# Converting the first dense group's third matrix between attention and its first product, and turning expert 0's rows three steps earlier

## The chip, the cores and the metric

The kernel runs on one core of a Trainium2 chip. The core has a matrix engine (TensorE, PE in the profile, with its weight loads shown as PEld), a vector engine (VectorE, DVE), an activation engine (ScalarE, ACT), a general engine (GpSimd, POOL) and SyncE (SP), which here only issues DMAs. Each engine works through its own instructions in order; semaphores make one wait for another. The metric is device time in microseconds of one launch; lower is better.

## The reference

Three parts follow each other: a masked attention, a dense gated layer, and a layer in which every token is sent to one of eight experts or to none.

```python
scores = scale * np.matmul(q, k.transpose(0, 1, 3, 2))        # 4 x 8 heads, 576 x 576, depth 64
mask_local = (rel >= 0) & (rel < 32)                          # heads 0 to 3
mask_strided = (rel >= 0) & (pos[None, :] % 32 == pos[:, None] % 32)   # heads 4 to 7
...
attn = attn / (np.sum(attn, axis=-1, keepdims=True) + 1e-09)
x = np.matmul(attn, v)                                        # then 2304 tokens x 512

gate = 1.0 / (1.0 + np.exp(-(x @ w_gate)))                    # w_gate, w_val 512 x 1536
x = gate * (x @ w_val) @ w_out                                # w_out 1536 x 512

do_compute = x @ w_skip > 0
e_idx = np.argmax(x[do_compute] @ w_gate8, axis=1)            # 8 experts
for e in range(8):
    h = np.maximum(xc[mask] @ w1[e], 0.0)                     # w1[e] 512 x 1024
    y[mask] = gate_w[mask, None] * (h @ w2[e])                # w2[e] 1024 x 512
out[do_compute] = xc + y
```

The three matrices of the dense layer arrive as 64-bit floats, everything else as 32-bit floats.

## The kernel before

All work is written in one fixed order by hand (a manual schedule): the order in which Python emits instructions is the order in which each engine does them. Waits follow from the tiles that are read and written, and from buffers that are used again.

**Precision.** A dense product is made of three: `mm3` (L434 to L436) multiplies high part by high part, high by low and low by high, so a weight and its operand each exist as `h` and `l` tiles (`whg`, `wlg` and so on; `xth`, `xtl` for the attention's result). The weights come as pairs of 32-bit words. `Weights.fetch(i)` (L382) loads one half of a 256 x 512 block (512 KB) by SP; `Weights.convert(i)` makes 32-bit floats of it in five DVE instructions (L396, L399, L402, L405, L409; tiles `cvg`, `cvv`, `cvo`), then ACT makes the high part (L417) and POOL subtracts to get the low part (L413). Since ACT and POOL are to come later in the order, these two are kept in the lists `after_act` and `after_pool` until a `flush`.

**Attention.** 32 steps (two query halves of two heads each) run as a pipeline that a string of letters sets in order: per step PE makes scores (L281), turns the probabilities (L328) and the next q or k (L222, L239) and applies v (L342); DVE, ACT and POOL do maxima, exponentials (L304), scaling (L319), and the high and low parts of the result (L350, L351, L362, L364). From step 13 on, PE also gets *fill* work: half a gated product of group 0 for units 0 to 2 (`gv_raw`, six `mm3` instructions each step). So `w_gate` and `w_val` of group 0 are fetched and converted in attention (letters L and D), and before the change `w_out` of group 0 is too: its halves are fetched at steps 13 and 14 and converted in the steps from 15 on.

**Dense layer.** The 2304 tokens are five units (four of 512, one of 256), the 1536 middle columns six groups of 256. `gv` makes the gate and value products of a unit and group, 48 instructions for two column blocks f; `glu` (L462, L463, L464, L467) makes `gt`, the gated product, in high and low part; `mout` multiplies by `w_out` (`who`, `wlo`) into `acc`. Right after attention come `glu_raw` for units 0 and 1 (sigmoid L506, product L507 on DVE, high part L509, low part L510 on POOL), `gv(0, 3)` for the fourth unit, then `mout` and `gv` in turn. A `tick` between output blocks moves one step of a later group's conversion.

**Choice and experts.** In the last group, each finished unit is turned back to rows (`turn_back`: L734, L735, L737, L738), its expert is chosen (`pick`, L747 to L775: nine small DVE instructions), and a step later its rows are scattered to `xs` by expert (`place`, L796). For the last unit (u = 4), the first 128 rows of expert 0 are fetched (`fetch`, L845, from units 0 to 2) and turned by `prep` (PE L872, ACT L874, DVE L876; tile `xx`) from within its second gated product: `route` is called after each of the four k steps of the gate (`g`) and value (`v`) product. The first expert products (`hide`, L998) and the last `mout` follow.

**Memory.** Pool `slab` has 30 buffers of 4 KB per partition, `slab2` 15 of them, in the memory that attention's tiles (masks, raw q and k, probabilities `pT`) leave.

Of the kernel before, what the change touches and what calls it, by code (L numbers as in the profile page):

```python
# [21 lines left out]
def kernel(  # L22
# [25 lines left out]
    G = 2  # L48
# [9 lines left out]
    NU = -(-NT // UT)  # L58
# [114 lines left out]
    def load_qk(b, ty, hp):  # L173
        if hp == 0:
            r = [att.tile([128, 2, 4, 2, D], F32, tag="raw", bufs=4, name=f"raw_{n}{b}{ty}") for n in "qk"]
            r.append(att.tile([128, 2, 2, D], F32, tag="rem", bufs=2, name=f"rem{b}{ty}"))
            raw_t[b, ty] = r
        r = raw_t[b, ty]
        h0 = 4 * ty + 2 * hp
        for i, src in enumerate((q, k)):  # L180
            for h in range(2):
                nc.sync.dma_start(
                    r[i][:, hp, :, h, :], src[b, h0 + h, 0:512, :].rearrange("(p r) d -> p r d", r=4)
                )
        for i, src in enumerate((q, k)):
            nc.sync.dma_start(
                r[2][64 * hp:64 * hp + 64, i], src[b, h0:h0 + 2, 512:S, :].rearrange("h p d -> p h d")
            )
# [24 lines left out]
    def turn(it, i, warm=0):  # L213
        b, ty, hp = it
        raw = raw_t[b, ty]
        if i == 0:
            kqs[it] = att.tile([128, 2, S], F32, tag="kq", bufs=3, name=f"kq{b}{ty}{hp}")
        kq = kqs[it]
        pt = bank([128, 4, 128], "Y")
        busy(warm, pt)  # L220
        for r in range(4):
            nc.tensor.transpose(pt[:, r, :], raw[i][:, hp, r].rearrange("p h d -> p (h d)"), ident)  # L222
        if ty == 0:
            dst = kq[:, i, 0:512].rearrange("p (c r) -> p c r", r=4)
            src = pt.rearrange("p r c -> p c r")
        else:
            dst = kq[:, i, :].rearrange("p (c r t) -> p c r t", r=4, t=TPC)[:, :, :, 0:16]
            src = pt.rearrange("p r (t c) -> p c r t", c=8)
        if i == 0:
            nc.vector.tensor_scalar(dst, src, SCALE, None, op0=ALU.mult)  # L230
        else:
            nc.scalar.copy(dst, src)
# [190 lines left out]
    after_act, after_pool, glus = [], [], []  # L423

    def flush(jobs):
        todo = list(jobs)
        jobs.clear()
        for job in todo:
            job()

    wt = {}
# [6 lines left out]
    def run(steps, n=99):  # L438
        for _ in range(n):
            if next(steps, 0) == 0:  # L440
                return
# [4 lines left out]
    def gv_mm(g, u, f, nm, tag, step=None):  # L446
        fs = slice(128 * f, 128 * f + 128)
        ps = bank([128, width(u)], tag)
        assert wt[g, nm].ready == 2
        whi, wlo = wt[g, nm].hi, wt[g, nm].lo  # L450
        for kk in range(KD):
            mm3(ps, whi[:, kk, fs], wlo[:, kk, fs], plane(xth[u], kk), plane(xtl[u], kk), kk == 0, kk == KD - 1)
            if step is not None:
                step(nm, kk)
        return ps

    def glu(g, u, f, pg, pvl):
        n = width(u)
        gt = slab2([128, 2, n], F32R, f"gt{g}{u}{f}")
        gts.setdefault((g, u), []).append(gt)  # L460
        sg = late.tile([128, UT], F32, tag="sg", bufs=2, name="sg")[:, 0:n]
        nc.scalar.activation(sg, pg, AF.Sigmoid)  # L462
        nc.vector.tensor_tensor(sg, sg, pvl, op=ALU.mult)  # L463
        nc.scalar.copy(gt[:, 0, :], sg)  # L464

        def low_part():
            nc.vector.tensor_tensor(gt[:, 1, :], sg, gt[:, 0, :].bitcast(F32), op=ALU.subtract)  # L467

        flush(glus)
        if f + 1 < G:  # L470
            glus.append(low_part)
        else:
            low_part()

    def gv_f(g, u, f, step=None):
        glu(g, u, f, *(gv_mm(g, u, f, nm, "ZY"[f], step) for nm in "gv"))

    def gv(g, u):
        for f in range(G):
            gv_f(g, u, f)  # L480

    def gv_raw(u, f, i):
        if i == 0:
            raws[u, f] = slab([128, 2, UT], F32, f"gvr{u}{f}")
        ps = bank([128, UT], "Z")
        w = wt[0, "gv"[i]]
        assert w.ready == 2
        fs = slice(128 * f, 128 * f + 128)
        for kk in range(KD):
            mm3(ps, w.hi[:, kk, fs], w.lo[:, kk, fs], plane(xth[u], kk), plane(xtl[u], kk), kk == 0, kk == KD - 1)  # L490
            if kk == 1:
                yield
        dst = raws[u, f][:, i, :]
        if i == 0:
            nc.vector.tensor_copy(dst, ps)
        else:
            nc.scalar.copy(dst, ps)  # L497
        yield

    def glu_raw(u):  # L500
        for f in range(G):
            raw = raws.pop((u, f))
            gt = slab2([128, 2, UT], F32R, f"gt0{u}{f}")
            gts.setdefault((0, u), []).append(gt)
            sg = raw[:, 0, :]
            nc.scalar.activation(sg, sg, AF.Sigmoid)  # L506
            nc.vector.tensor_tensor(sg, sg, raw[:, 1, :], op=ALU.mult)  # L507
            yield
            nc.scalar.copy(gt[:, 0, :], sg)  # L509
            nc.gpsimd.tensor_tensor(gt[:, 1, :], sg, gt[:, 0, :].bitcast(F32), op=ALU.subtract)  # L510
            yield
# [31 lines left out]
    load_qk(0, 1, 0)  # L543
    load_v(0, 0)
    load_qk(0, 1, 1)
    for nm in "gvo":
        wt[0, nm] = Weights(0, nm, slab, slab)
    ADD = 20
    NRAW = 3
    FILL = {}  # L550
    FILL0 = 13
    BUSY = ((1, 2), (1, 2), (1, 2), (1, 2), (0, 1), (0, 1), (0, 1), (0, 1), (0, 1), (0, 0), (0, 1), (0, 1), (1, 1), (1, 1), (0, 1), (1, 0))
    FETCH = (5, 6, 7, 8, 13, 14)
    halves = [x for u in range(NRAW) for i in range(2) for f in range(G) for x in [gv_raw(u, f, i)] for _ in range(2)]
    for i, x in enumerate(halves):
        FILL.setdefault(min(FILL0 + i, NS + 2), []).append(x)
    early = [(nm, i) for nm in "gvo" for i in range(2)]
    turn(items[0], 0, 8)
    turn(items[0], 1, 1)
    cq = []  # L560
# [59 lines left out]
    def step_loads(t):  # L620
# [16 lines left out]
        if 17 <= t < 23:  # L637
            late_consts(t - 17)
        if t in FETCH:
            nm, i = early[FETCH.index(t)]  # L640
            wt[0, nm].fetch(i)
        if t - 2 in FETCH:
            nm, i = early[FETCH.index(t - 2)]
            cq.append(wt[0, nm].convert(i))
# [24 lines left out]
    def slab2(shape, dt, name):  # L669
        return late.tile(shape, dt, tag="slab2", bufs=NSLAB2, name=name)  # L670
# [236 lines left out]
    for g in range(1, NG):  # L907
        for nm in "gvo":
            plan(g, nm)
    todo = [glu_raw(u) for u in range(NRAW)]  # L910
    for n in range(2 * G):
        for u in range(2):
            run(todo[u], 1)
    gv(0, NRAW)
    for u in range(NU):

        def between(d, u=u):
# [7 lines left out]
    for g in range(1, NG):  # L925
        last = g == NG - 1
        for u in range(NU):
            if g == 2:
                init_xs(u)
            if not last:  # L930
                gv_f(g, u, 0)
                if u > 0:
                    mout(g, u - 1, ticks)
                elif g > 1:
                    mout(g - 1, NU - 1, ticks)
                gv_f(g, u, 1)
                continue
            steps = back = picks = iter(())

            def seat(nm, kk):  # L940
                nonlocal steps
                if u > 1 and (nm, kk) == ("g", 1):
                    steps = place(u - 2, rank_sums(rst[u - 2][1], "X"))
                run(steps, 1)

            gv_f(g, u, 0, seat)
            run(steps)
            if u == 0:
                w_e0.append(load_e(0, 0))
            if u == NU - 1:  # L950
                xg, ins = fetch(0, PARTS[:1])
                tc.add_to_no_dep_group("head", ins.ins)
            if u > 0:
                mout(g, u - 1, part(u - 1))
                back = turn_back(u - 1)
                picks = pick(u - 1)
            else:
                mout(g - 1, NU - 1, ticks)

            def route(nm, kk):  # L960
                if u == NU - 1 and (nm, kk) == ("v", 3):
                    pp.extend(prep(0, xg, PARTS[:1], tag="Z", gates=False))
                if nm == "g":
                    run(back, 2)
                else:
                    run(picks, 4)

            gv_f(g, u, 1, route)
            run(picks)
            for i in {0: (1, 2), 1: (3, 4), 2: (5, 6), 3: (7,)}.get(u, ()):  # L970
                w_e0.append(load_e(0, i))
# [15 lines left out]
    pending, jobs = [], []  # L987
# [297 lines left out]
```

## Time and profile before

| | |
|---|---|
| median of 3 runs | 789.06 us (784.98 to 790.59) |
| profiled execution | 785.84 us, its span 784.1 us |
| PE busy | 757.9 us, 97% of the span |
| DVE, ACT, POOL busy | 487.9, 345.2, 261.6 us |
| granted TensorE clock, mean | 0.994 |

The span runs from the first to the last instruction; the rest of the profiled execution's time lies around it. A busy PE does not mean that PE is at its peak: instructions overlap, and one of 128x512 is listed with 0.39 us where the next begins 0.23 us later. What tells are the places where PE waits, and for whom. All times of rows are from the start of the span.

### The profile page before, as it was taken

How to read it: one execution, taken by the hardware profiler on the slowest of the kernel's cores; microseconds unless marked ns; L12 is line 12 of the kernel's file. 1: busy time of each engine (PE TensorE's matmuls, PEld its weight loads, DVE VectorE, ACT ScalarE, POOL GpSimd, SP SyncE). 2: the span in 40 equal slices, each digit the busy share in tenths (PEclk: the TensorE clock that was granted, in tenths of full speed). 3: DMA queues.
4: the chain of work that ended last, by engine and by line, in shares of the span. 5: the costliest groups of instructions: out<-in, count | busy, mean ns of one | idle time of the engine just before them, and what ended most of it. 6: DMA issues, size and time to landing. Idle time of an engine off the chain costs nothing. (4 is left out here: it accounts for less than half of the span.)

```text
span 784.1 us, 12866 instructions
## 1 busy us (share of the span) xinstructions
PE 757.9 (97%) x4522; PEld 629.0 (80%) x4524; DVE 487.9 (62%) x1130; ACT 345.2 (44%) x1001; POOL 261.6 (33%) x259
## 2 busy tenths in 40 slices
PE   8989999999999999999999999999999999999994
PEld 5757677688888888888888888888888888888882
DVE  4698876469465574575466457277775776665650
ACT  5877679565211221222111212344444755666530
POOL 5565643253111011011011101424424456665610
PEclk9999999999999999999999999999999999999998
DMA  6988451213101333011002000223346766666600
GB/s 162 212 208 220 105 117 32 81 28 108 54 29 52 110 96 122 28 54 54 27 28 81 28 27 27 71 97 135 109 145 185 254 231 234 233 234 207 215 28 13
DMA packets 86447, 87.82 MB, mean 112 GB/s; under 512 B 55991, under 2 KB 58551, under 8 KB 86376
## 3 DMA queue, kind: packets, MB, share of 16 engines
q1 hardware_dynamic: 81032, 76.45, 32.4%
q0 software_dynamic: 3616, 7.33, 2.7%
q10 hardware_dynamic: 1728, 3.15, 1.1%
q8 instruction: 38, 0.62, 0.4%
q14 instruction: 33, 0.27, 0.1%
HBM read 73.48 MB, written 19.28 MB: 118 GB/s over the span
## 5 line engine op out<-in xcount | busy, mean ns | idle before, releaser
L435 PE MATMUL psX<-gt,who 128*128 128x512 f32 (+1 forms) x240 | 88.4, 369 | 0.0
L434 PE MATMUL psX<-gt,who 128*128 128x512 f32 (+1 forms) x240 | 88.4, 368 | 0.0
L464 ACT CAST gt<-sg 128x512 fp32r<-128x512 f32 (+1 forms) x54 | 30.9, 572 | 130.3 <-DVE sg L463 128.8
L436 PE MATMUL psX<-gt,wlo 128*128 128x512 f32 (+1 forms) x240 | 88.3, 368 | 0.0
L319 POOL TENSOR_TENSOR sm<-sm,rs 96x384 f32<-96x384 f32 (+2 forms) x64 | 51.0, 816 | 66.4 <-DVE rs L313 37.0
L528 DVE TENSOR_TENSOR acc<-psX,acc 128x512 f32<-128x512 f32 (+1 forms) x100 | 62.8, 631 | 11.6 <-PE psX L436 11.4
L463 DVE TENSOR_TENSOR sg<-sg,psZ 128x512 f32<-128x512 f32 (+1 forms) x27 | 17.0, 628 | 67.4 <-PE psZ L436 65.8
L413 POOL TENSOR_TENSOR wlv<-cvv,whv 128x512 fp32r<-128x512 f32 x12 | 17.0, 1415 | 113.9 <-ACT whv L417 113.9
L436 PEld LDWEIGHTS psX<-gt,wlo 128*128 128x128 f32 x240 | 45.2, 188 | 7.6
L434 PEld LDWEIGHTS psX<-gt,who 128*128 128x128 f32 x240 | 45.2, 189 | 7.5
L435 PEld LDWEIGHTS psX<-gt,who 128*128 128x128 f32 x240 | 45.2, 188 | 7.5
L434 PE MATMUL psZ<-xth,whv 128*128 128x512 f32 (+1 forms) x132 | 50.3, 381 | 0.9 <-ACT gvr L497 0.7
L434 PE MATMUL psZ<-xth,whg 128*128 128x512 f32 (+1 forms) x132 | 50.3, 381 | 0.0
L436 PE MATMUL psZ<-xth,wlv 128*128 128x512 f32 (+1 forms) x132 | 49.2, 373 | 0.0
L435 PE MATMUL psZ<-xtl,whv 128*128 128x512 f32 (+1 forms) x132 | 49.1, 372 | 0.0
L436 PE MATMUL psZ<-xth,wlg 128*128 128x512 f32 (+1 forms) x132 | 49.0, 371 | 0.0
L435 PE MATMUL psZ<-xtl,whg 128*128 128x512 f32 (+1 forms) x132 | 49.0, 371 | 0.0
L463 DVE TENSOR_TENSOR sg<-sg,psY 128x512 f32<-128x512 f32 (+1 forms) x27 | 17.0, 628 | 47.9 <-PE psY L436 45.7
L1076 POOL DMA_INDIRECT out_dram<-xg x16 | 21.1, 1321 | 75.1 <-DVE xg L1075 40.4
L413 POOL TENSOR_TENSOR wlo<-cvo,who 128x512 fp32r<-128x512 f32 x12 | 17.4, 1450 | 83.4 <-ACT who L417 83.4
L467 DVE TENSOR_TENSOR gt<-sg,gt 128x512 fp32r<-128x512 f32 (+1 forms) x54 | 34.0, 630 | 17.1 <-ACT gt L464 16.6
L413 POOL TENSOR_TENSOR wlg<-cvg,whg 128x512 fp32r<-128x512 f32 x12 | 18.4, 1531 | 71.8 <-ACT whg L417 55.2
(748 smaller groups left out, 2244.5 us busy)
## 6 DMA issues: line engine op xcount, KB each, us to landing
w1r<-in_moe_w_dram SPq DMA_DIRECT2D x32, 512.0 KB
w2r<-in_moe_w_dram SPq DMA_DIRECT2D x32, 512.0 KB
wg<-in_moe_w_gate_dram SPq DMA_DIRECT2D x12, 512.0 KB
wv<-in_moe_w_val_dram SPq DMA_DIRECT2D x12, 512.0 KB
wo<-in_moe_w_out_dram SPq DMA_DIRECT2D x12, 512.0 KB
raw_q<-in_q_dram SPq DMA_DIRECT2D x32, 128.0 KB
raw_k<-in_k_dram SPq DMA_DIRECT2D x32, 128.0 KB
xs<-zero SPq DMA_DIRECT2D x14, 260.5 KB
```

The costliest lines, as they stand in the source:

```text
L319: nc.gpsimd.tensor_tensor(x, x, rs[:n, h, 0:m].rearrange("p (w o) -> p w o", o=1).to_broadcast([n, m, c]), op=ALU.mult)
L413: nc.gpsimd.tensor_tensor(l, wf, h.bitcast(F32), op=ALU.subtract)
L434: nc.tensor.matmul(ps, lhsT=whi, rhs=xhi, start=start, stop=False)
L435: nc.tensor.matmul(ps, lhsT=whi, rhs=xlo, start=False, stop=False)
L436: nc.tensor.matmul(ps, lhsT=wlo, rhs=xhi, start=False, stop=stop)
L463: nc.vector.tensor_tensor(sg, sg, pvl, op=ALU.mult)
L464: nc.scalar.copy(gt[:, 0, :], sg)
L467: nc.vector.tensor_tensor(gt[:, 1, :], sg, gt[:, 0, :].bitcast(F32), op=ALU.subtract)
L528: nc.vector.tensor_tensor(ac, po, ac, op=ALU.add)
L1076: nc.gpsimd.indirect_dma_start(out=out[:, :], out_offset=bass.IndirectOffsetOnAxis(ap=xg[t][:n, TW - 1:TW].bitcast(I32), axis=0), in_=y, i ...
```

## The change

Two things move. First, `w_out` of group 0 is no longer fetched and converted in attention. It is fetched right after attention (into `slab2` buffers, with `row` buffers as scratch), and its conversion runs step by step while the fourth unit's gated products `gv(0, 3)` are emitted: `turn_o` flushes the ACT and POOL lists and moves the conversion one step after each of the 16 k steps. The two DVE, ACT and POOL parts that are left are flushed behind it. Second, for the last unit the turning of expert 0's first rows (`prep`) is called after the first k step of the value product, not after the fourth; the four calls to `pick` of the unit before (the fourth unit) lie behind it now.

```diff
@@ -543,18 +543,18 @@
     load_qk(0, 1, 0)
     load_v(0, 0)
     load_qk(0, 1, 1)
-    for nm in "gvo":
+    for nm in "gv":
         wt[0, nm] = Weights(0, nm, slab, slab)
     ADD = 20
     NRAW = 3
     FILL = {}
     FILL0 = 13
     BUSY = ((1, 2), (1, 2), (1, 2), (1, 2), (0, 1), (0, 1), (0, 1), (0, 1), (0, 1), (0, 0), (0, 1), (0, 1), (1, 1), (1, 1), (0, 1), (1, 0))
-    FETCH = (5, 6, 7, 8, 13, 14)
+    FETCH = (5, 6, 7, 8)
     halves = [x for u in range(NRAW) for i in range(2) for f in range(G) for x in [gv_raw(u, f, i)] for _ in range(2)]
     for i, x in enumerate(halves):
         FILL.setdefault(min(FILL0 + i, NS + 2), []).append(x)
-    early = [(nm, i) for nm in "gvo" for i in range(2)]
+    early = [(nm, i) for nm in "gv" for i in range(2)]
     turn(items[0], 0, 8)
     turn(items[0], 1, 1)
     cq = []
@@ -908,10 +908,23 @@
         for nm in "gvo":
             plan(g, nm)
     todo = [glu_raw(u) for u in range(NRAW)]
+    wt[0, "o"] = Weights(0, "o", slab2, slab3)
+    for i in range(2):
+        wt[0, "o"].fetch(i)
+    first_o = chain(wt[0, "o"].convert(0), wt[0, "o"].convert(1))
+
+    def turn_o(nm, kk):
+        flush(after_pool)
+        flush(after_act)
+        run(first_o, 1)
+
     for n in range(2 * G):
         for u in range(2):
             run(todo[u], 1)
-    gv(0, NRAW)
+    for f in range(G):
+        gv_f(0, NRAW, f, turn_o)
+    for jobs in (after_act, after_pool):
+        flush(jobs)
     for u in range(NU):
 
         def between(d, u=u):
@@ -958,7 +971,7 @@
                 mout(g - 1, NU - 1, ticks)
 
             def route(nm, kk):
-                if u == NU - 1 and (nm, kk) == ("v", 3):
+                if u == NU - 1 and (nm, kk) == ("v", 0):
                     pp.extend(prep(0, xg, PARTS[:1], tag="Z", gates=False))
                 if nm == "g":
                     run(back, 2)
```

On DVE, between attention and the first `mout`, the order before reads as follows (`gvr` is a raw product of `gv_raw`, `sg` the gate of unit 3, `cvg` a conversion for group 1):

```order
L507 TENSOR_TENSOR gvr_1200<-gvr_1200 128x512
L507 TENSOR_TENSOR gvr_1804<-gvr_1804 128x512
L463 TENSOR_TENSOR sg<-sg,psZ 128x512
L463 TENSOR_TENSOR sg<-sg,psY 128x512
L467 TENSOR_TENSOR gt_2525<-sg,gt_2525 128x512
L467 TENSOR_TENSOR gt_2556<-sg,gt_2556 128x512
L396 TENSOR_SCALAR cvg_2579<-wg_2573 128x512
```

The same place on DVE now (`cvo` and `wo` are the third matrix):

```order
L507 TENSOR_TENSOR gvr_1782<-gvr_1782 128x512
L396 TENSOR_SCALAR cvo_2487<-wo_2457 128x512
L399 SCALAR_TENSOR_TENSOR cvo_2487<-wo_2457,cvo_2487 128x512
L402 SCALAR_TENSOR_TENSOR cvo_2487<-wo_2457,cvo_2487 128x512
L405 TENSOR_SCALAR wo_2457<-wo_2457 128x512
L409 SCALAR_TENSOR_TENSOR cvo_2487<-wo_2457,cvo_2487 128x512
L396 TENSOR_SCALAR cvo_2510<-wo_2459 128x512
L399 SCALAR_TENSOR_TENSOR cvo_2510<-wo_2459,cvo_2510 128x512
L402 SCALAR_TENSOR_TENSOR cvo_2510<-wo_2459,cvo_2510 128x512
L463 TENSOR_TENSOR sg<-sg,psZ 128x512
L405 TENSOR_SCALAR wo_2459<-wo_2459 128x512
L409 SCALAR_TENSOR_TENSOR cvo_2510<-wo_2459,cvo_2510 128x512
```

All ten conversion instructions stand behind the last L507, and the first L463 has moved into the second half of them.

On DVE in the last group's last unit, around the choice (L747 to L775) of the unit before, the order before ends the choice like this:

```order
L773 TENSOR_TENSOR eq<-eq,rmx 128x32
L775 TENSOR_TENSOR oh_all<-eq,va 128x32
L876 TENSOR_TENSOR xx_6072<-psZ,xx_6072 128x2x128
L876 TENSOR_TENSOR xx_6073<-psZ,xx_6073 128x2x128
L463 TENSOR_TENSOR sg<-sg,psY 128x256
L467 TENSOR_TENSOR gt_6084<-sg,gt_6084 128x256
```

The same place now:

```order
L876 TENSOR_TENSOR xx_6038<-psZ,xx_6038 128x2x128
L876 TENSOR_TENSOR xx_6039<-psZ,xx_6039 128x2x128
L747 TENSOR_TENSOR lg<-lp 128x40
L759 TENSOR_REDUCE rmx<-lg 128x4
L761 TENSOR_SCALAR va<-lg 128x4
L763 TENSOR_TENSOR eq<-lg,rmx 128x32
L765 TENSOR_TENSOR lm_all<-lg,rmx 128x32
L767 TENSOR_TENSOR eq<-eq,desc 128x32
L771 TENSOR_REDUCE rmx<-eq 128x4
L773 TENSOR_TENSOR eq<-eq,rmx 128x32
L775 TENSOR_TENSOR oh_all<-eq,va 128x32
L463 TENSOR_TENSOR sg<-sg,psY 128x256
```

The two L876 of expert 0's rows have moved from behind the choice to ahead of it; L463 and L467 of the last unit still follow the choice.

On PE at the same place, now:

```order
L735 MATMUL psX<-wri,sl_5918 128x138
L434 MATMUL psY<-xth_2090,whv_4681 128x256
L435 MATMUL psY<-xtl_2091,whv_4681 128x256
L436 MATMUL psY<-xth_2090,wlv_4682 128x256
L872 MATMUL psZ<-ident,xg_5912 128x128 x4
L434 MATMUL psY<-xth_2090,whv_4681 128x256
```

Nine products of the value's remaining k steps come behind the transposes L872; they stood ahead of them.

## Rows read from the trace of the kernel before

**Rows 1.** Who PE waited for, 60 to 100 us: total, times, longest.
```profile
PE psY L239 <- DVE xtl L364: 1.2, 1, 1.2
```

**Rows 2.** Timeline, POOL and DVE in attention: start, us, engine, line.
```profile
86.67 1.48 POOL L413 TENSOR_TENSOR wlo<-cvo,who 128x512 fp32r<-128x512 f32 x1
87.02 1.67 DVE L409 SCALAR_TENSOR_TENSOR cvo<-wo,cvo 128x512 f32<-128x512 int32 x1
88.62 0.76 DVE L364 TENSOR_TENSOR xtl<-psY,xth 128x252 fp32r<-128x252 f32 x2
```

**Rows 3.** Windows: length, busy of the five engines, granted clock, DMA share, GB/s.
```profile
91.70:95.10 3.40, 3.40 (x17) 2.89 (x16) 2.42 (x12) 2.24 (x13) 2.24 (x4) 0.50 0.00 0
```

**Rows 4.** Timeline of PE: starts of fill groups.
```profile
86.63 0.48 PE L434 MATMUL psZ<-xth,whv 128*128 128x512 f32 x1
...
98.20 0.48 PE L434 MATMUL psZ<-xth,whg 128*128 128x512 f32 x1
...
106.51 0.48 PE L434 MATMUL psZ<-xth,whg 128*128 128x512 f32 x1
```

**Rows 5.** Timeline of PE: first and sixth instruction of the first `mout`.
```profile
165.14 0.39 PE L434 MATMUL psX<-gt,who 128*128 128x512 f32 x1
...
166.27 0.39 PE L436 MATMUL psX<-gt,wlo 128*128 128x512 f32 x1
```

**Rows 6.** Timeline of DVE and POOL after attention; x2 merges two instructions, and windows overlap.
```profile
159.53 2.40 DVE L507 TENSOR_TENSOR gvr<-gvr 128x512 f32<-128x512 f32 x2 [1.27 <-ACT gvr L506]
159.65 3.44 POOL L510 TENSOR_TENSOR gt<-gvr,gt 128x512 fp32r<-128x512 f32 x2
161.35 3.00 POOL L510 TENSOR_TENSOR gt<-gvr,gt 128x512 fp32r<-128x512 f32 x2
163.17 0.69 DVE L463 TENSOR_TENSOR sg<-sg,psZ 128x512 f32<-128x512 f32 x1 [1.24 <-ACT sg L462]
```

**Rows 7.** A later conversion on DVE with POOL beside it; last, all copies L417 of `who`.
```profile
187.32 0.42 DVE L396 TENSOR_SCALAR cvo<-wo 128x512 int32<-128x512 int32 x1
187.77 0.69 DVE L399 SCALAR_TENSOR_TENSOR cvo<-wo,cvo 128x512 int32<-128x512 int32 x1
188.62 1.74 POOL L413 TENSOR_TENSOR wlv<-cvv,whv 128x512 fp32r<-128x512 f32 x1 [2.23 <-ACT whv L417]
189.11 1.54 DVE L405 TENSOR_SCALAR wo<-wo 128x512 int32<-128x512 int32 x1
L417 ACT CAST who<-cvo x4: 618/622/632, 82.5 to 195.4; 128x512 fp32r<-128x512 f32 x4
```

**Rows 8.** Window with two fetches of group 1 landing; attention's last product on PE.
```profile
151.00:152.00 1.00, 1.00 (x6) 0.80 (x5) 0.00 (x0) 0.00 (x0) 0.00 (x0) 1.00 1.05 406
...
153.40 0.78 PE L342 MATMUL psY<-pT,v 108*64 108x108 f32 x12
```

**Rows 9.** Timeline of PE and its weight loads in the last group's last unit.
```profile
578.99 0.28 PE L436 MATMUL psY<-xth,wlv 128*128 128x256 f32 x1
580.33 0.42 PEld L872 LDWEIGHTS psZ<-ident,xg 128*128 128x128 f32 x4 [0.20 <-DMA xg<-xs]
582.18 0.39 PE L998 MATMUL psY<-xx,w100h 128*128 128x256 f32 x1 [1.20 <-DVE xx L876]
583.74 0.39 PE L435 MATMUL psX<-gt,who 128*128 128x256 f32 x1
```

**Rows 10.** Timeline of DVE and ACT at the same place.
```profile
579.54 0.20 DVE L747 TENSOR_TENSOR lg<-lp 128x40 f32<-128x40 f32 x1
...
580.89 0.19 DVE L775 TENSOR_TENSOR oh_all<-eq,va 128x32 bf16<-128x32 f32 x1
582.37 0.41 DVE L463 TENSOR_TENSOR sg<-sg,psY 128x256 f32<-128x256 f32 x1
582.82 0.41 ACT L464 CAST gt<-sg 128x256 fp32r<-128x256 f32 x1 [0.86 <-DVE sg L463]
583.25 0.43 DVE L467 TENSOR_TENSOR gt<-sg,gt 128x256 fp32r<-128x256 f32 x1 [0.47 <-ACT gt L464]
```

## The prediction

> **What bounds the kernel now.** TensorE (PE) sets the end. I read first who PE waited for: over the whole span only a few waits reach 1 us. So an edit gains only where it removes a PE wait, and costs only where it makes one. I then read the two places that the change touches, engine by engine, in order of time, and the granted clock beside them.
>
> The first place is the stretch of attention in which `wo` of group 0 is converted. PE's longest wait there, 1.2 us, is for VectorE's (DVE's) L364 [rows 1]. That L364 starts at 88.62 because the conversion's last step, L409, lies before it on DVE: L409 came at 87.02, took 1.67 us, and ended 0.54 us after GpSimd's (POOL's) L413, which had started first and ran from 86.67 to 88.15 [rows 2]. Shortly after this standstill PE runs at the lower of its two clock levels: the granted clock is 0.50 (1.2 GHz) from 91.7 to 95.1 [rows 3].
>
> The second place is the moment at which PE needs `who` and `wlo`. It reads the first half of `who` at 165.14 and the second half of `wlo` at 166.27, and waits for neither [rows 5]: both were done in attention.
>
> **The change part by part.**
>
> *Removed from attention: gain 3.3 us.* From the fill group that begins at 86.63 to the second one behind it, at 98.20, PE took 11.57 us; for the next two, with the same kinds of work between them, it took 8.31 (98.20 to 106.51) [rows 4]. The difference, 3.26, holds the standstill and the slow clock together. At worst only the 1.2 us wait goes away; at best 3.5, with small waits that I don't count. I take 3.3, since both steps consist of the same instructions. Ten DVE instructions, two ACT copies, two POOL subtractions and two 512 KB fetches leave this stretch; the q, k and v loads that SP issued behind them come sooner, and nobody waits long for those, so I count nothing for that. What is late next there is PE's own issue.
>
> *Added between attention and the first `mout`: PE stands still 7.4 us.* The order shows the ten conversion instructions on DVE behind all four L507. The fourth L507 ends at 161.93 (159.53 plus 2.40), and POOL runs L510 without a pause until 164.35: the third of its four starts at 161.35 and ends at 163.09 (159.65 plus 3.44) [rows 6]. PE wants the result 3 to 4 us later. What DVE and POOL do to each other is in rows: POOL's L413 ran from 188.62 to 190.36, and DVE's L405, which came at 189.11 and takes 0.42 alone like L396, ended at 190.65, 0.29 after it [rows 7]; L409 above ended 0.54 after. POOL's operation took 1.74 there instead of about 1.3, because DVE was busy when it came. So, one by one, in the time of the old trace:
>
> - L396 waits for the third L510: 163.09 plus 0.28 is 163.4. The fourth L510 then runs to about 164.6. L399 waits for it: 165.15.
> - L402 (0.69), L405 (0.42) and L409 (0.69) follow free: 166.9 (the durations: [rows 7]).
> - ACT copies the first half of `who` in 0.62 [rows 7]: 167.6. POOL makes the first half of `wlo`, 1.7 with DVE busy: 169.35.
> - Second half on DVE: L396 and L399 to 167.95; L402 is held until `wlo` is done, 169.9; then L463 (0.69 [rows 6]), which stands in the middle of this half, 170.5; L405 and L409 to 171.6.
> - ACT 172.3, POOL 1.3 to 1.4: 173.7.
>
> PE's sixth instruction of `mout` needs this: 173.7 less 166.27 is 7.4 us. In that time PE has five instructions. DVE, ACT and POOL come out of it as far ahead of PE as before, so nothing is given back later. Bounds: if POOL never held DVE, the first half would be ready on DVE at 164.8 and the last step 3.2 us earlier, 4.2; if every step of the second half were held as well, about 8.2.
>
> The page SBUF — State Buffer of the Trainium skill (Who interferes with whom) has the two engines share a port pair as an exclusive lock: the later instruction fully blocks until the first is finished. By that, a held L405 would end its whole 0.42 after POOL's end and a held L409 its 0.69, where the rows show 0.29 and 0.54; over the three held steps of the chain the standstill would be 0.4 longer and the forecast 795.2. I stay with the rows. The same rule speaks against putting a DVE conversion beside POOL's four L510 at all.
>
> *The fetches: nothing.* The first needs the mask's memory, free before the end of attention. The second needs memory that the last attention product still reads, and so is issued at about 154.2 (L342, 153.40 plus 0.78); at the 406 GB/s that SP's queue reached a little earlier, its 512 KB take 1.3 us plus some start-up [rows 8]. DVE comes to it at about 166.9, and the `wg` and `wv` fetches behind it on SP are wanted later still. If that cover were gone, the cost would be added to the 7.4.
>
> *Slow clock after this standstill: 1.7 us.* Five instructions in more than 8 us is less work than PE had in the stretch ahead of 91.7. The row of 91.7 to 95.1 prices one slow stretch: 3.4 us at half speed, 1.7 lost [rows 3]. Bounds 0 (the slow stretch lies inside the standstill) and 3.4 (a second follows); I take one.
>
> *Expert 0's rows turned nine instructions earlier: 1.6 us lost.* The transposes (L872) did not start when PE was free but 0.20 us later, at 580.33, when the rows had landed [rows 9]. The fetch's issue is not moved. So behind the third product of `v` (578.99) PE now waits about 1.1 us for the same landing. That alone costs little: the nine products (1.1 us) fill the 1.2 us in which PE waited for L876 before L998 at 582.18 [rows 9]. But on DVE the two L876 now stand ahead of the choice. The nine instructions of the choice took 579.54 to 581.08, in a time in which DVE had nothing else; now they come behind L876, from about 582.4, where L463 stood [rows 10]. L463 starts at about 583.95, ends at 584.35, ACT's L464 (0.41) ends at 584.8, L467 (0.43) at 585.3. PE's second `mout` product with this tile stood at 583.74 [rows 9]: 1.6 late. Bounds: if the rows landed 1.1 us sooner the choice would start sooner too and the cost is 0 or a gain of some tenths; with a slow clock behind it, 3.3.
>
> *Sum:* -3.3 + 7.4 + 1.7 + 1.6 = +7.4 us. On the profiled execution, 785.84: 793.2. That execution is one of the fast ones: the median of the three runs is 3.2 above it. I add half of that and predict 794.8.
>
> **The rivals.**
>
> *Hidden conversion, not slower.* The place is DVE ahead of the first `mout`. If DVE took the conversion while PE was in the fourth unit's 48 products, the 3.3 stay and only the tail counts: -1.7, 785.7 with the same half added. Decisive is whether the first L396 starts before about 154.5 (7.4 us before 161.9). For it speaks that PE works some 11 us between attention and `mout`; against it, that four L507, each behind an ACT step, stand ahead of it on DVE. Chance 0.06.
>
> *No holding by POOL.* The standstill is 4.2, the clock costs half, the tail is as above: +3.4, 790.8. Against it stand [rows 2, 7]. Chance 0.12.
>
> *Clock falls twice, slower by over 1%.* A second slow stretch, either behind the standstill of 7.4 us or in the tail, where PE now stands twice within 6 us for 1.1 and 1.6 us: +1.7 or, with both, +3.4, so 796.5 to 798.2. Decisive is how much PE does in the stretch before. Against the tail: a wait of 1.2 us at 582 left the clock alone. Chance 0.37.
>
> My forecast has the rest, 0.45.
>
> **How the numbers follow.** About 1% is what a measurement of this kernel can tell from no change. The forecast, 7.4 us, is 0.9% of the mean of the two bases, just inside; the error of the sum (some 1 us) and of a median of runs that spread over 5.6 us put part of it outside, and part of the double-clock case inside. So slower 0.40, within 1% 0.54, faster 0.06. The range takes in the case without holding and the two clock cases with the scatter of the runs: 789.5 to 800; the likeliest case alone is 792 to 797.
>
> **What would show it.** Right: no conversion in attention, fill groups near 4.2 us throughout and no half clock at 92; PE waiting at the first `mout` for `who` from ACT and `wlo` from POOL, some 7 us in total, longer than any wait of before; a stretch of 0.50 behind it; PE waiting about 1 us for `xg` and 1.6 us for the last unit's `gt`. Wrong: conversion steps on DVE that don't stretch while POOL runs; rows of expert 0 that land before the transposes; a half clock in attention that stays although the standstill is gone.

## The result, and the profile after

The changed kernel takes 793.64 us (median of 11 runs, 791.9 to 797.49), the kernel before 785.82 (11 runs, 784.5 to 790.67): ratio 1.0103, 95% interval 1.0081 to 1.0124, which is 8.1 us slower (the medians differ by 7.8). The profiled execution took 797.33 us, its span 795.6; mean granted clock 0.979. Of the 11 executions of the changed kernel four, the profiled one among them, took 796.68 to 797.49 us at a mean granted clock of 0.979 to 0.981, the other seven 791.9 to 794.11 at 0.987 to 0.992.

Who PE waited for in the changed kernel, from 155 to 185 us and from 570 to 600 us (total, times, longest; what is left out waits 0.5 us or less):

```profile
PE psX L434 <- ACT who L417: 4.4, 2, 2.3
PE psX L436 <- POOL wlo L413: 0.4, 1, 0.4
...
PE psZ L872 <- DMA xg<-xs: 1.1, 1, 1.1
PE psX L434 <- ACT gt L464: 1.0, 1, 1.0
```

None of these four stood there before; the 1.2 us for L364 in attention [rows 1] and the 1.2 at L998 [rows 9] are gone. PE's timeline of the changed kernel: two fill groups (answering to 86.63 and 98.20 in [rows 4]), the last product of `gv(0, 3)`, the fourth and sixth of the first `mout` ([rows 5]), and the first of the fifth unit:

```profile
87.06 0.48 PE L434 MATMUL psZ<-xth,whv 128*128 128x512 f32 x1
...
95.25 0.48 PE L434 MATMUL psZ<-xth,whg 128*128 128x512 f32 x1
...
162.01 0.39 PE L436 MATMUL psY<-xth,wlv 128*128 128x512 f32 x1
...
169.12 0.79 PE L434 MATMUL psX<-gt,who 128*128 128x512 f32 x1 [2.07 <-ACT who L417]
...
170.47 0.79 PE L436 MATMUL psX<-gt,wlo 128*128 128x512 f32 x1
...
177.08 0.28 PE L434 MATMUL psZ<-xth,whg 128*128 128x256 f32 x1
```

The fill groups lie 8.19 us apart, 11.57 before. PE could have begun `mout` 0.23 us after 162.01, and in the kernel before the sixth instruction came 1.13 us behind the first [rows 5], so here it could have come at 163.37. It comes at 170.47, 7.1 us later; I call this the standstill. The list above has 4.8 us of it, since it counts only time in which no instruction is listed; in the rest the first five instructions start further apart than before. They are listed with up to 0.79 us in place of 0.39, and the windows (as in [rows 3]) show half the clock, from the time when PE begins again until 175 us, and once more behind the tail. I call such a stretch at 0.50 a half clock.

```profile
164.00:165.00 1.00, 0.28 (x1) 0.29 (x2) 0.96 (x3) 0.95 (x2) 0.26 (x1) 0.92 0.00 0
...
165.00:170.00 5.00, 2.52 (x5) 0.91 (x4) 3.75 (x6) 1.90 (x4) 2.06 (x2) 0.50 0.00 0
...
175.00:176.00 1.00, 1.00 (x6) 0.82 (x5) 0.33 (x1) 0.10 (x1) 0.95 (x1) 0.96 0.00 0
...
602.00:603.00 1.00, 1.00 (x10) 0.91 (x10) 0.22 (x2) 0.27 (x1) 0.99 (x5) 0.50 0.85 224
```

The conversion on DVE in the changed kernel, and POOL beside it (start, us):

```profile
155.54 6.12 POOL L510 TENSOR_TENSOR gt<-gvr,gt 128x512 fp32r<-128x512 f32 x4 [12.07 <-ACT gt L509]
159.01 1.51 DVE L396 TENSOR_SCALAR cvo<-wo 128x512 int32<-128x512 int32 x1
160.56 1.66 DVE L399 SCALAR_TENSOR_TENSOR cvo<-wo,cvo 128x512 int32<-128x512 int32 x1
162.25 0.69 DVE L402 SCALAR_TENSOR_TENSOR cvo<-wo,cvo 128x512 int32<-128x512 int32 x1
...
164.74 1.47 POOL L413 TENSOR_TENSOR wlo<-cvo,who 128x512 fp32r<-128x512 f32 x1 [3.07 <-ACT who L417]
165.11 1.65 DVE L402 SCALAR_TENSOR_TENSOR cvo<-wo,cvo 128x512 int32<-128x512 int32 x1
167.73 0.69 DVE L409 SCALAR_TENSOR_TENSOR cvo<-wo,cvo 128x512 f32<-128x512 int32 x1
169.15 1.28 POOL L413 TENSOR_TENSOR wlo<-cvo,who 128x512 fp32r<-128x512 f32 x1 [2.94 <-ACT who L417]
```

Each step that meets POOL takes 1.5 to 1.7 us, each other 0.42 or 0.69. In the tail, PE and DVE (answering to [rows 9, 10]):

```profile
586.88 0.66 PE L872 MATMUL psZ<-ident,xg 128*128 128x128 f32 x4 [1.09 <-DMA xg<-xs]
588.25 0.76 DVE L876 TENSOR_TENSOR xx<-psZ,xx 128x256 fp32r<-128x256 f32 x2 [2.22 <-ACT xx L874]
588.93 0.19 DVE L747 TENSOR_TENSOR lg<-lp 128x40 f32<-128x40 f32 x1
...
590.38 0.41 DVE L463 TENSOR_TENSOR sg<-sg,psY 128x256 f32<-128x256 f32 x1
591.28 0.38 PE L434 MATMUL psX<-gt,who 128*128 128x256 f32 x1 [1.00 <-ACT gt L464]
```

The choice (L747 on) begins when L876 is done, and L463 waits for the choice to end.

**Where the 11.5 us of the two profiled spans come from.** I subtract the starts of the same PE instruction in the two traces; plus means later in the changed kernel. It is +0.78 at 82 us (it has a half clock at 42 to 45 us that the trace of before lacks, and a longer wait near 49), -2.89 when `gv(0, 3)` begins, +6.49 behind the first `mout`, +6.52 up to the last unit, +8.00 at its last `mout`, +11.39 at the end. So attention gave 3.7, the first `mout` took 9.4, the tail 1.5, and the stretch behind it 3.4, in which the half clock at 598 to 609 lies.

### The profile page after: what moved, and what is told of

Its sections match the earlier page's. It is cut to its first block, busy times and chain, and to the rows that moved or that the text cites. A ratio compares the mean times of both kernels' runs of the same rounds, so it can differ in the third digit from the quotient of the medians.

```text
span 795.6 us, 12870 instructions
## 1 busy us (share of the span) xinstructions
PE 767.2 (96%) x4524; PEld 635.5 (80%) x4524; DVE 488.1 (61%) x1130; ACT 346.3 (44%) x1001; POOL 260.0 (33%) x259
## 5 line engine op out<-in xcount | busy, mean ns | idle before, releaser
L434 PE MATMUL psX<-gt,who 128*128 128x512 f32 (+1 forms) x240 | 90.0, 375 | 5.4 <-ACT who L417 4.4
L436 PE MATMUL psX<-gt,wlo 128*128 128x512 f32 (+1 forms) x240 | 89.8, 374 | 0.6 <-POOL wlo L413 0.4
L435 PE MATMUL psX<-gt,who 128*128 128x512 f32 (+1 forms) x240 | 89.6, 373 | 0.1
L319 POOL TENSOR_TENSOR sm<-sm,rs 96x384 f32<-96x384 f32 (+2 forms) x64 | 49.9, 799 | 68.1 <-DVE rs L313 42.2
L528 DVE TENSOR_TENSOR acc<-psX,acc 128x512 f32<-128x512 f32 (+1 forms) x100 | 62.9, 632 | 11.6 <-PE psX L436 11.4
L463 DVE TENSOR_TENSOR sg<-sg,psZ 128x512 f32<-128x512 f32 (+1 forms) x27 | 17.0, 629 | 66.4 <-PE psZ L436 66.4
L413 POOL TENSOR_TENSOR wlv<-cvv,whv 128x512 fp32r<-128x512 f32 x12 | 16.9, 1409 | 113.9 <-ACT whv L417 113.9
L436 PEld LDWEIGHTS psX<-gt,wlo 128*128 128x128 f32 x240 | 45.9, 191 | 9.7 <-POOL wlo L413 2.0
L436 PE MATMUL psZ<-xth,wlg 128*128 128x512 f32 (+1 forms) x132 | 49.0, 371 | 0.0
L436 PE MATMUL psZ<-xth,wlv 128*128 128x512 f32 (+1 forms) x132 | 49.0, 371 | 0.0
L463 DVE TENSOR_TENSOR sg<-sg,psY 128x512 f32<-128x512 f32 (+1 forms) x27 | 17.0, 629 | 49.1 <-PE psY L436 46.4
L413 POOL TENSOR_TENSOR wlo<-cvo,who 128x512 fp32r<-128x512 f32 x12 | 17.4, 1450 | 89.4 <-ACT who L417 89.4
L467 DVE TENSOR_TENSOR gt<-sg,gt 128x512 fp32r<-128x512 f32 (+1 forms) x54 | 34.1, 631 | 17.0 <-ACT gt L464 16.6
L413 POOL TENSOR_TENSOR wlg<-cvg,whg 128x512 fp32r<-128x512 f32 x12 | 18.4, 1535 | 73.0 <-ACT whg L417 73.0
```

The lines of the kernel that those rows point to most:

```text
L319: nc.gpsimd.tensor_tensor(x, x, rs[:n, h, 0:m].rearrange("p (w o) -> p w o", o=1).to_broadcast([n, m, c]), op=ALU.mult)
L413: nc.gpsimd.tensor_tensor(l, wf, h.bitcast(F32), op=ALU.subtract)
L434: nc.tensor.matmul(ps, lhsT=whi, rhs=xhi, start=start, stop=False)
L435: nc.tensor.matmul(ps, lhsT=whi, rhs=xlo, start=False, stop=False)
L436: nc.tensor.matmul(ps, lhsT=wlo, rhs=xhi, start=False, stop=stop)
L528: nc.vector.tensor_tensor(ac, po, ac, op=ALU.add)
```

## The experiments

All were timed against the kernel before on the same chip; its median was 784.4 to 786.0. The offsets (us, plus is later) are those of the paragraph above, from one profiled execution each, with the half clocks that this one had. "Mout" is a late product of group 0's turn (before: 247.26), "tail" the last unit's last `mout` (586.32).

| version | ratio, 95% interval | gv(0,3) | mout | tail | end |
|---|---|---|---|---|---|
| changed kernel | 1.0103, 1.0081 to 1.0124 | -2.9 | +6.5 | +8.0 | +11.4 |
| e1_matrix_only | 1.0079, 1.0047 to 1.0110 | -3.7 | +5.4 | +5.6 | +7.0 |
| e2_rows_only | 1.0023, 1.0000 to 1.0046 | -1.4 | -1.4 | +1.5 | +3.1 |
| e3_pool_free | 1.0073, 1.0047 to 1.0099 | -3.6 | +2.4 | +4.7 | +8.3 |
| e4_later_in_attention | 0.9995, 0.9974 to 1.0015 | 0.0 | 0.0 | 0.0 | +1.9 |
| e6_choice_first | 1.0002, 0.9985 to 1.0018 | -1.7 | -1.7 | -1.6 | -2.1 |
| e7_conversion_first | 1.0120, 1.0092 to 1.0147 | -2.9 | +7.1 | +7.1 | +6.6 |
| e8_busy_pe | 1.0089, 1.0063 to 1.0115 | -3.9 | +3.4 | +5.9 | +5.7 |
| e9_steps_24_25 | 1.0049, 1.0027 to 1.0070 | -1.0 | -1.0 | -0.9 | +2.4 |
| e10_unit1_in_gv | 1.0099, 1.0069 to 1.0129 | -4.0 | +3.6 | +4.1 | +7.5 |
| e11_units_spread | 1.0061, 1.0041 to 1.0081 | -3.0 | +3.0 | +3.1 | +2.9 |
| e12_fifth_unit_first | 1.0024, 1.0003 to 1.0045 | -3.0 | +1.6 | +1.8 | +1.3 |
| e13_only_order | 1.0045, 1.0025 to 1.0065 | -3.6 | +3.3 | +3.2 | +2.7 |

### Each part alone

The changed kernel with the call of `prep` at `("v", 3)` again:

> The third matrix moved as in the change, expert 0's rows turned behind the fourth k step as before. Theory (two parts that add, the first the larger): about 3.5 us come back in attention and some 9.3 are lost at the first mout (7.2 standing, 2.1 at the slow clock), so 5.7 us slower than the kernel before, and the tail as before, with one wait of 1.2 us at L998 and no slow clock behind it. Rival (the turned rows carry most of the loss): under 3 us slower.

The kernel before with that call at `("v", 0)`:

> Only expert 0's rows turned ahead of the choice; the third matrix is converted in attention as before. Theory: 1.5 us slower than the kernel before, all of it PE's wait for the last unit's gt, since the choice lies behind L876 on DVE; in some executions 3.4 more, when the clock falls behind the two waits. Rival (the wait for the rows only takes the place of the one for L876, and the choice costs nothing): within 0.5 us of the kernel before.

The matrix alone costs 6.2 us by the ratio, the rows alone 1.8; together 8.0, the change 8.1, each with an interval of about 2 us to either side. In e1 attention gave 3.7 and the first `mout` took 9.2, and in the tail only 0.1 changed. In e2 the tail took 3.0, some 1.5 of it by a half clock (584 to 587 us). So the first theory holds. The ratio of e2 (0.0 to 3.6 us) would allow its rival too; it is e2's trace, and the next experiment, that speak for its theory. In e2's attention nothing was changed, and still it lies 1.6 us better from 86.63 to 98.20: the half clock of [rows 3] did not come in that execution.

### The tail: the choice or the wait

The kernel before with

```diff
-                if u == NU - 1 and (nm, kk) == ("v", 3):
+                if u == NU - 1 and (nm, kk) == ("v", 0):
+                    run(picks)
                     pp.extend(prep(0, xg, PARTS[:1], tag="Z", gates=False))
```

> The kernel before, with expert 0's rows turned after the first k step of the value product, but with all of the choice emitted ahead of them, so that DVE's order is that of the kernel before and only PE's transposes move. Theory (the loss in the tail comes from the choice standing behind L876 on DVE, not from PE's wait for the rows): PE waits about 1.1 us for the rows in place of 1.2 at L998, none for gt, and the first product behind the tail comes within 0.3 us of where it stood; total within 0.5 us of the kernel before. Rival (PE's earlier wait is what costs): the tail 1.5 us longer, as in the changed kernel.

PE waits as long for the rows, and for nothing else for longer than before:

```profile
PE psZ L872 <- DMA xg<-xs: 1.2, 1, 1.2
```

The tail takes 0.1 us more than before, and the time is the same. So what the turned rows cost is the choice behind L876 on DVE; PE's earlier wait only takes the place of that at L998.

### What makes the conversion late

The changed kernel, in `glu_raw`, without POOL's subtraction for units 0 and 1 (it leaves out the low parts of these products):

```diff
+            if u < 2:
+                nc.vector.memset(gt[:, 1, :].bitcast(F32), 0.0)
             nc.scalar.activation(sg, sg, AF.Sigmoid)
...
-            nc.gpsimd.tensor_tensor(gt[:, 1, :], sg, gt[:, 0, :].bitcast(F32), op=ALU.subtract)
+            if u >= 2:
+                nc.gpsimd.tensor_tensor(gt[:, 1, :], sg, gt[:, 0, :].bitcast(F32), op=ALU.subtract)
```

> The changed kernel without POOL's four L510 ahead of the conversion: the low parts of the products of units 0 and 1 in group 0 are left out (filled with zeros by DVE while it waits for ACT). Theory (POOL holds DVE): L507 takes some 0.69 us each in place of 1.23 in the second pair, L396 0.42 in place of 1.51, the first L399 0.69 in place of 1.66; the conversion ends 3.4 us sooner, and the time is 3.4 to 5 us under the changed kernel's. Rival (POOL holds nothing, DVE's steps are long for another reason): the steps keep their 1.5 to 1.7 us, and the time is within 0.5 us of the changed kernel's.

DVE in this run, and the first POOL instruction near it:

```profile
158.11 0.41 DVE L396 TENSOR_SCALAR cvo<-wo 128x512 int32<-128x512 int32 x1
158.56 0.69 DVE L399 SCALAR_TENSOR_TENSOR cvo<-wo,cvo 128x512 int32<-128x512 int32 x1
...
161.78 1.47 POOL L413 TENSOR_TENSOR wlo<-cvo,who 128x512 fp32r<-128x512 f32 x1 [19.00 <-ACT who L417]
162.15 1.65 DVE L402 SCALAR_TENSOR_TENSOR cvo<-wo,cvo 128x512 int32<-128x512 int32 x1
```

L396 and L399 take 0.41 and 0.69 with POOL idle, in place of 1.51 and 1.66; the L402 that still meets L413 keeps its 1.65. So POOL does hold DVE. The theory's 3.4 us for the conversion was too much: counted from `gv(0, 3)`, the second `wlo` is done 2.3 us sooner, and the standstill is 4.9 us in place of 7.1. The half clock is shorter as well (166 to 170), so that from `gv(0, 3)` to behind the first `mout` this run loses 6.0 us, the changed kernel 9.4. At the end the ratio has 2.4 us of these 3.4, under the 3.4 to 5 expected, and its interval overlaps that of the changed kernel; its trace has two more half clocks, at 590 to 593 and 600 to 607.

The changed kernel with products in PE's standstill; `warm(k)` emits k products of 128x512 into a bank that nobody reads, and the three products of `mm3` are written out here, so that L436 becomes L536:

```diff
...
+                    warm((10, 11)[f])
+                    nc.tensor.matmul(po, lhsT=ohi[:, f, ds_], rhs=h, start=(f == 0), stop=False)
+                    nc.tensor.matmul(po, lhsT=ohi[:, f, ds_], rhs=l, start=False, stop=False)
+                    warm((4, 0)[f])
...
```

> The changed kernel with 25 further products of 128x512, into a bank that nobody reads, in the places where PE stands still at the first mout (10, 4 and 11 of them); nothing is left out. Theory (the standstill lowers the clock, and that costs 2.1 to 2.3 us on top of it): the granted clock stays at 1.00 from 160 to 176 us, the eighth product row of mout comes 2.1 to 2.3 us sooner than in the changed kernel, and the time is 2 us under it. Rival (the clock falls there for another reason, or the extra products take PE longer than it would have waited): a stretch of 0.50 in spite of them, and the time within 0.5 us of the changed kernel's, or above.

Its windows view for the same five microseconds, and its sixth instruction:

```profile
165.00:170.00 5.00, 4.38 (x18) 2.93 (x17) 3.78 (x7) 2.36 (x4) 1.51 (x2) 1.00 0.00 0
...
169.51 0.50 PE L536 MATMUL psX<-gt,wlo 128*128 128x512 f32 x1 [0.62 <-POOL wlo L413]
```

The last product of `gv(0, 3)` began at 161.02 here, so the standstill, now filled, is still 7.1 us, but the clock stays at 1.00: from the sixth instruction to the fifth unit's first product it takes 4.4 us (to 173.94), against 6.6 in the changed kernel. So the half clock costs 2.2 us, and it comes from PE's standing still: with PE busy it is gone, while e1 and e3, which keep the standstill, have it too (164 to 174 and 166 to 170). Of the 2 us expected in the whole time the ratio shows 1.1, and the two intervals overlap; the trace lost 1.2 us between 530 and 570 us, for which I have no cause.

### Other places in attention

The kernel before with `FETCH = (5, 6, 7, 8, 21, 22)` (e4), and with 24 and 25 at the end (e9):

> The kernel before with the third matrix fetched at steps 21 and 22 of attention in place of 13 and 14, so that it is converted from step 23 on. Theory (in attention the conversion cost 3.7 us only because it met a crowded DVE and POOL near 87 us; later DVE is busy half the time): 3 to 3.7 us faster than the kernel before, no half clock near 92 us, no wait at the first mout. Rival (the conversion costs PE that much wherever it lies in attention): within 0.7 us of the kernel before, with a new wait of over 1 us behind step 23.

> The kernel before with the third matrix fetched at steps 24 and 25 of attention. At steps 21 and 22 the conversion cost PE 3.0 us where it lay, against 3.7 at steps 13 and 14. Theory now (it costs where its last step, held by POOL, stands ahead of an L364 that PE waits for; with DVE busy 2.4 to 2.6 of each 4 us from 123 us on, against 2.3 to 3.6 before that, there is less of it): it costs 1 to 2 us near 125 to 140, so 783.5 to 785 in all. Rival (it costs about 3 us at any place of attention): within 0.7 us of the kernel before.

My theory fell in e4, and the rival came. The old place was 3.7 us shorter, and the new one 3.0 longer. Its windows, with a DVE row and the PE wait behind it:

```profile
119.00:123.00 4.00, 3.08 (x27) 2.61 (x28) 3.93 (x12) 3.85 (x16) 2.95 (x3) 1.00 0.27 83
123.00:127.00 4.00, 2.56 (x29) 1.64 (x28) 3.97 (x22) 2.47 (x10) 1.31 (x3) 1.00 0.00 0
...
122.24 1.67 DVE L409 SCALAR_TENSOR_TENSOR cvo<-wo,cvo 128x512 f32<-128x512 int32 x1
...
124.65 0.72 PE L342 MATMUL psY<-pT,v 128*64 128x96 f32 x12 [0.90 <-DVE xtl L364]
```

DVE is full there, and again an L409 of 1.67 us stands ahead of an L364 for which PE waits, the pattern of [rows 2]; another 1.3 us of waiting there is for POOL's L319. At steps 24 and 25 the loss is 2.6 us, and the pattern is another: the longest wait is for ACT's L332, 1.9 us. So that theory fell too. By the ratio e9 is 3.8 us slower than before, more than its rival allowed; in its trace a half clock at 590 to 600 us lies behind the tail. The half clock near 92 us is no fixed part of the price: e4 lost its 3.0 at a clock of 1.00.

### Attempts to make room for it

In the expectations of this section, "the last version" and "two versions ago" mean e7, and "the version beside it" means e10.

e7, from the changed kernel with `prep` as before, and unit 1's and 2's products from `between`, a unit ahead of the `mout` that reads them:

```diff
-    for n in range(2 * G):
-        for u in range(2):
-            run(todo[u], 1)
+    run(first_o, 2)
+    run(todo[0], 1)
+    run(first_o, 3)
+    run(todo[0], 2)
+    flush(after_act)
+    run(todo[0], 1)
...
-            if u + 2 < NRAW:
-                next(todo[u + 2])
+            if u + 1 < NRAW:
+                next(todo[u + 1])
```

> The third matrix moved as in the change, but its first half is converted right after attention, between the two products of unit 0, the second half behind them, and unit 1's two L507 and L510 come only while unit 0's mout runs; expert 0's rows as before. Theory (PE stands still because the conversion is queued behind four L507 on DVE and collides with four L510 on POOL): both halves are ready some 6 us sooner, PE stands still 1 to 2 us in place of 7.1, the clock stays high or falls for one stretch; of the 3.7 us from attention 1.5 to 3.5 remain, so 782.5 to 784.5 against 786 of the kernel before. Rival (DVE, ACT and POOL have no room there, so the wait only moves): PE waits as long for unit 1's gated product at the second mout, and the time stays over 788.

The first `mout` now loses 1.8 us, as the theory said, but the waits move behind it (160 to 250 us):

```profile
PE psX L435 <- POOL gt L510: 3.8, 3, 2.2
PE psX L436 <- POOL wlo L413: 0.6, 1, 0.6
PE psX L434 <- ACT who L417: 0.5, 1, 0.5
```

With a half clock from 186 to 192 us behind them it is as slow as the change. So the rival was right too. The next two spread these products: in e10 unit 1's over the second block of `gv(0, 3)`, in e11 half of them there and half in the first `mout`, and unit 2's over `gv(0, 4)` (lines of e11, both on top of e7's early conversion):

```diff
+        if kk == 0:
+            run(todo[1], 1)
...
+            for f in range(G):
+                gv_f(0, u + NRAW + 1, f, turn_2)
```

> The last version of the conversion right after attention, but unit 1's two L507 and L510 come while PE is in the second block of the fourth unit's gated products, unit 2's in unit 0's mout as in the changed kernel. Theory (DVE, ACT and POOL have room for all of it from 155 to 190 us; the last version only ran two units' products straight ahead of the mout that reads them): PE stands still 1.8 us at the first mout, under 1 us at the second and third, no slow clock; 3.7 less 1.8 to 2.8 leaves 0.9 to 1.9 us under the kernel before. Rival (there is no room, the wait moves again): waits of over 3 us in all between 160 and 200 us, and over 2 us slower than the kernel before.

> As the version beside it, with unit 1's products half in the fourth unit's second block and half in unit 0's mout, and unit 2's in the fifth unit's gated products. Theory: as for the version beside it, with no wait at the second and third mout; 1.5 to 2 us under the kernel before. Rival (no room): waits of over 3 us in all between 160 and 200 us, and over 2 us slower than the kernel before.

Both theories miss, and both rivals come. The longest wait is now for the bank `psX`. ACT's L526 frees it, and that stands behind the inserted products on ACT: 4.1 us in all in e10, 3.0 in e11:

```profile
PE psX L434 <- ACT acc L526: 4.1, 1, 4.1
...
PE psX L434 <- ACT acc L526: 3.0, 3, 1.5
```

Last, the fifth unit's `gv(0, 4)` ahead of all `mout`s: in e13 that alone (its lines are shown), in e12 with e7's early conversion and with unit 1's products inside `gv(0, 4)`:

```diff
+    gv(0, NRAW + 1)
...
-        if u + NRAW + 1 < NU:
-            gv(0, u + NRAW + 1)
```

> The conversion's first half between unit 0's two products as two versions ago, two steps of its second half ahead of the fourth unit's L463, and the fifth unit's gated products ahead of all of group 0's mouts (unit 1's products while they run, unit 2's in unit 0's mout); expert 0's rows as in the kernel before. Theory (PE stands still because the conversion's result is wanted too soon, and 5.6 us of other products are there to put in between): no wait of 1 us or more for the third matrix at the first mout, no slow clock near it, and the 3 to 3.7 us from attention remain: 781.5 to 783 against 785 of the kernel before. Rival (DVE, ACT and POOL are full, the wait moves to the banks or to a unit's gated product): waits of over 2 us in all from 160 to 200 us, no faster than the kernel before.

> The third matrix moved as in the change, with nothing but the fifth unit's gated products put ahead of group 0's mouts; expert 0's rows as before. Theory (the same, but the fourth unit's L462 and L463 stand among the late conversion, and the fifth unit's products need the banks that these free): PE waits 2 to 3 us for the banks at 162 us and about 1 more at the first mout, in place of 7.2 for the third matrix, with no slow clock or one short stretch; within 1 us of the kernel before. Rival (the third matrix is that late whatever stands between): over 3 us slower than the kernel before.

In e12 PE waits nowhere for the third matrix and the clock stays up, but ACT's L526 is late four times:

```profile
PE psX L434 <- ACT acc L526: 2.7, 4, 1.5
```

It loses 4.6 us between `gv(0, 3)` and the late product, more than these 2.7. Each of the four waits costs some 0.27 us that the list does not count: instructions overlap by 0.16 us where PE does not wait (listed with 0.39, the next 0.23 later), and the first behind a wait takes 0.50. Two pauses too short for the list, near 172 and 175 us, cost 0.7. In e13 the loss is 6.9, with 2.8 us of waiting for L462 and a half clock at 166 to 170. Both theories miss again, and both rivals come. e12 is the nearest, and is still 0.24% slower than the kernel before (0.03 to 0.45). So the third matrix cost PE 2.6 us or more at every other place tried; at its old one it costs 3.7, or 2.1 where the half clock doesn't come.

## Why the prediction was right

*Attention, -3.3.* Measured 3.4 between the two fill groups, 3.7 with the group ahead of them. But 1.6 of it is a half clock that e2 and e6, with the attention of the kernel before, did not have: I had priced a disturbance of one execution as a fixed gain. The terms as measured add up to 7.2 with it and 8.8 without, and the 8.1 lie between; that the sum came so near is in this part luck.

*Standstill, +7.4.* Measured 7.1. Nobody waited for the fetches, as forecast. Step by step in the time of the old trace (add 2.9 to the new): L399 done 165.1 (said 165.15), first half of DVE 166.9 (166.9), first half of `wlo` 169.1 (169.35), end 173.3 (173.7). That POOL holds DVE is shown by e3. By the rule in the Trainium skill's page SBUF — State Buffer (Who interferes with whom), that the later instruction fully blocks, it would have been 0.4 more. The trace doesn't agree in this: L399 ended 0.56 us after POOL's last L510, and the second L402 0.55 after L413, not 0.69.

*Slow clock, +1.7.* Right mechanism, as e8 shows; 2.2 to 2.3 in size. The clock fell when PE began again and stayed down until 175, 10.2 us in place of the 3.4 that I had priced, but only the last 4.6 of these lie behind the standstill.

*Tail, +1.6.* Measured 1.5, and e6 shows the cause that the prediction gave. (The list has 1.0 us of waiting for `gt` and not 1.6, as it counts idle time only.)

*The base.* The sum of 793.2 on the profiled execution lies 0.4 from the median measured. The 1.6 that I added for the median of three runs was not needed: over 11 runs the median of before, 785.82, is the profiled execution's own time.

*The rivals.* A second slow clock, the largest of them, came in the profiled execution (598 to 609 us, 3.4 us). By time and mean clock only three others of the 11 were like it; the median execution, at 0.987, does not seem to have it. That it belongs to the change is not shown: e4, e9 and e10, whose tail is that of the kernel before, have a half clock there as well (from 596, 590 and 594 us), while e8, with the tail of the change, has none.

## What to carry to other kernels

A conversion that is moved out of a full stretch must be followed to the engine that does it: what stands ahead of it in that engine's queue, and what the neighbouring engine does meanwhile, gave this standstill to within half a microsecond. Where three helpers feed PE in turn, an order that removes one of PE's waits can make the next one visible (here `who`, then `gt`, then the bank behind L526), so price the whole stretch, not the wait. A half clock in one trace is to be checked against a second trace before its end is counted as a gain.

## What the runs showed that I had not expected

Half clocks turn up where nothing was edited: at 42 to 45 us in the changed kernel, e7, e11 and e12 (43 to 49 in e4), not in the kernel before, e1 or e2. In the five kernels that had one, PE is 0.7 us later at 82 us than in the kernel before. And DVE's L697 in the tail, with the same instructions ahead of it, waits very differently. In the kernel before, and in e1:

```profile
593.98 0.17 DVE L697 TENSOR_TENSOR sl<-psY,base_e 128x16 f32<-128x16 f32 x1 [0.63 <-PE psY L683]
...
600.98 0.17 DVE L697 TENSOR_TENSOR sl<-psY,base_e 128x16 f32<-128x16 f32 x1 [2.06 <-PE psY L1011]
```

In e1 PE then waited 1.3 us for DVE at 601.5, and that is the 1.4 us by which e1 falls back behind the tail. PE had done L697's products by 598.85. e2 has the same (DVE idle for 2.06 us, PE then for 1.3). What held DVE is open; no run was made for it.
